# Three shifted sums by accumulating DMA, and three more kv transforms with eight residues

## The chip, the cores and the metric

The kernel runs on one core of a Trainium2 chip. The metric is the device time of one execution in microseconds (us). A core has TensorE (PE: matmuls and transposes, which write to PSUM), VectorE (DVE), ScalarE (ACT) and GpSimd (POOL), each with its own list of instructions, worked off in order, and SyncE (SP), which issues DMAs. DMAs are also issued by ScalarE and GpSimd.

## The reference

A forward pass and all its gradients. `x` is 2048 x 1024, the gated unit has 3584 columns.

```python
k_shift = sum(k_pad[:, t:t + S, :] * shift_k[:, ks - 1 - t] for t in range(4))   # four taps
kv = k_shift * v
y = irfft(rfft(pad(kv)) * rfft(pad(ssm_k))) [:S] + kv * ssm_D                    # long convolution
s = xn * y                                                                       # xn = layernorm(x)
g = silu(((xn @ w_gate) * (xn @ w_up)) @ w_down)
out = x + s * g
# returned: out and the gradients of all nine inputs for a given grad_out
```

What the change touches is the first two lines, the shifted sum `k_shift` and its product with `v`, and the transform of kv.

## The kernel before, in words

The kernel is one long stream for TensorE: layer norm and transposes of x; the gate and up projections in 14 slabs of 256 columns (`gu_unit`, line 655, matmuls at L671); the down projection (L1034); the backward products of the gated unit (L1482, L1499, L1582, L1644). The long convolution runs beside it as a generator, `conv_forward` (line 740), for the forward pass and another for the backward pass. The generator yields after each step, with a weight in us of VectorE's work less most of the TensorE time that the step adds. After each gate-up piece (eight 128x512 matmuls, one PSUM tile `psg`, two buffers) `tick` calls `pump`, which draws steps of the generator until their weights reach the share of a planned total `F_TOTAL` (line 925) that the tick stands for. So the planner's total and the weights set where each step of the convolution stands in the lists of all engines.

The forward convolution works on eight slices `ds` of 128 channels. For each slice there is a *kv* input (16 rows of 128 x 128) and a *filter* input `hx`. Both are transformed by a short transform across residues and matmuls with tables `TF`. A transform consists of two *halves*. A half is a set of matmuls at L234 into two PSUM tiles `psF` (two buffers), which ScalarE copies to a tile `SP` (two buffers, one for each half). VectorE then combines them (`W<-SP` and so on) to the spectrum, `KX` for kv and `HX` for the filter. There are two forms:

- four residues: `fwd4_half`, 16 matmuls of 128x256 a half, ScalarE copies at L256, and on VectorE `fwd4_sums` and `fwd4_outs`, eight operations of 128x1024;
- eight residues: `fwd8_half` (line 287), 8 matmuls of 128x256 a half, ScalarE copies at L295, and on VectorE `fwd8` (line 297), with more sums and four multiply-adds (L283).

`EIGHT` (line 732) lists which transforms take the second form, as pairs of slice and kind (0 is kv, 1 the filter). Slice 0 transforms the filter first, every later slice kv first. A slice then runs so: kv transform, filter transform, turn of the filter spectrum (`turned`), the product of the two spectra (`product`, five steps), the inverse (`inv8` or `inv_dft`), into which the two kv halves of the next slice are laid (`ahead`). The filter halves are laid into the kv transform. The matmuls of the inverse (L455, `psI<-HX,TI`) are laid into the next slice's second transform; those of slice 7 follow the 63rd and the 70th of a counted row of the down projection's matmuls (`late_mm`).

Kv itself is made for two slices at a time by `shift(dp)`, dp from 0 to 3: eight VectorE operations of 128 x 4096 bf16. The sum is in `U[6]`, the product of the moment in `U[7]`, k in `krow`, v in `U[4]`:

```python
tt(acc, k[:, :, 0:8, :], wb(3), MUL)
for j in (2, 1, 0):
    tt(prod, k[:, :, 3 - j:11 - j, :], wb(j), MUL)
    tt(acc, acc, prod, ADD)
tt(kv, acc, v, MUL); st(KSHd[dp], acc)
```

`shift(0)` stands ahead of all slices. `shift(1)`, `shift(2)` and `shift(3)` stand behind the product of slices 1, 3 and 5, and the loads of k and v for them at the start of these slices (`load_kv`, eight DMAs on GpSimd's queue). VectorE's instructions keep the order of the program here (`PIN`). `st` and `cld` issue DMAs from GpSimd, `ld` from SyncE, `sta` from ScalarE. Every VectorE operation by the helper `tt` has line L212, and every store by `st` L66. The other VectorE work of this stage is `hN<-gut`, the product of gate and up, once in four gate-up pieces.

An accumulating DMA is there in one place already: four DMAs of 1 MB at L1550 add A_q to out_0, both in DRAM.

In the backward stage `dw_slab` (line 1495) copies weight gradients to tiles `wb` (three buffers) and stores them.

Of the kernel before, what the change touches and what calls it, by code (L numbers as in the profile page):

```python
# [13 lines left out]
BF16 = mybir.dt.bfloat16  # L14
F32 = mybir.dt.float32
# [4 lines left out]
def build_kernel(  # L20
# [39 lines left out]
    def ld(out, in_):  # L60
        return nc.sync.dma_start(out=out, in_=in_)
# [49 lines left out]
    Hd = dram.tile([NSL, P, 2, NB, P], BF16, name="Hd")  # L111
    HTd = [[dram.tile([4, P, n, 256], BF16, name=f"HTd{i}{j}") for j, n in enumerate((8, 8, 8, 4))] for i in range(2)]
    DGd = dram.tile([NSL, 2, S, SLW], BF16, name="DGd")


    const = ctx.enter_context(tc.tile_pool(name="const", bufs=1))
# [94 lines left out]
    def tt(o, a, b, op):  # L211
        pinned(V.tensor_tensor(o, a, b, op))  # L212
# [439 lines left out]
    chunk = [0]  # L652
    mate = []

    def gu_unit(sl, b0, n, w, tick):

        if n == 4:
            turn_of[0] += 1
            if turn_of[0] % 3 == 0 and sl < NSL - 2:
                gut = U[5][:, 2048:4096].rearrange("p (a i f) -> p a i f", a=2, i=4)  # L660
            else:
                gut = fg.tile([P, 2, 4, SLW], BF16, name="gut")
            hN = fg.tile([P, 2, 4, P], BF16, name="hN", bufs=3)
        else:
            gut = lnp.tile([P, 2, 2, SLW], BF16, name="gut_s", bufs=6)
            hN = lnp.tile([P, 2, 2, P], BF16, name="hN_s", bufs=6)
        for i in range(n):
            q, qi = divmod(b0 + i, 4)
            ps = ps_gu.tile([P, 512], F32, name="psg")
            for dc in range(DC):  # L670
                gu_mm[0] = nc.tensor.matmul(ps[:], XNT[q][:, dc, qi * P:(qi + 1) * P],  # L671
                                            w[:, dc].rearrange("p a f -> p (a f)"), start=(dc == 0), stop=(dc == DC - 1))
            nc.scalar.copy(out=gut[:, :, i], in_=ps[:].rearrange("p (a f) -> p a f", a=2))  # L673
            flush(5)
            if i == 0:
                turn_late()
            hn[0]()
            hn[0] = nop
            tick()
        sta(GUd[sl, b0 // 8][:, :, b0 % 8:b0 % 8 + n], gut[:, :, 0:n])  # L680

        def multiply():
            with tc.issue_after(last.ins) if b0 + n <= 4 and chunk[0] <= 2 else nullcontext():
                by_half = lambda t: t.rearrange("p i (a f) -> p a i f", a=2)
                tt(hN[:, :, 0:n], by_half(gut[:, 0, 0:n]), by_half(gut[:, 1, 0:n]), MUL)
            st(Hd[sl][:, :, b0:b0 + n, :], hN[:, :, 0:n])
            if sl < 2:
                defer(turn)
            else:
                mate.append(hN)  # L690
                if b0 % 8 == 4:
                    defer(turn_pair)
        hn[0] = multiply

        def turn_pair():
            hT = fg.tile([P, 4, 2, 2, P], BF16, name="hT", bufs=1)
            two_, mate[:] = mate[0:2], mate[2:]
            ps = tr_tile()[:].rearrange("p h b x -> p h (b x)").rearrange("p h (b u) -> p h b u", u=64)
            for qq in range(4):
                for a in range(2):  # L700
                    for i in range(2):
                        turn_halves(lambda hh: ps[:, hh, 4 * qq + 2 * a + i], two_[qq // 2][:, a, qq % 2 * 2 + i, :])
            to = HTd[b0 // 8][sl // 4][:, :, 2 * (sl % 4):2 * (sl % 4) + 2, :]
            for g in range(2):
                nc.scalar.copy(out=halves(hT[:, 2 * g:2 * g + 2].rearrange("p q a i s -> p (q a i) s")), in_=ps[:, :, 8 * g:8 * g + 8])
            ht_st[0] = ld(to.rearrange("q f a s -> f q (a s)"), hT[:].rearrange("f q a i s -> f q (a i s)"))

        def store(hT):
            half, rest = divmod(b0, 8)
            q0, i0 = divmod(rest, 2)  # L710
            to = HTd[half][sl // 4][:, :, 2 * (sl % 4):2 * (sl % 4) + 2, :]
            if n == 4:
                ht_st[0] = ld(to[q0:q0 + 2].rearrange("q f a s -> f q (a s)"), hT.rearrange("f q a i s -> f q (a i s)"))
            else:
                ht_st[0] = ld(to[q0, :, :, i0 * P:(i0 + n) * P], hT[:, 0, :, 0:n].rearrange("f a i s -> f a (i s)"))

        def turn():
            hT = fg.tile([P, 4, 2, 2, P], BF16, name="hT", bufs=1)[:, 0:2] if chunk[0] > 5 else lnp.tile([P, 2, 2, 2, P], BF16, name="hT_s", bufs=5)[:]
            ps = tr_tile()[:, 0].rearrange("p (q a i) x -> p q a i x", q=2, a=2)
            for a in range(2):  # L720
# [8 lines left out]
    h_out = []  # L729
    cv_gone = []  # L730
    ht_st = [None]
    EIGHT = ((0, 0), (0, 1), (6, 0), (7, 0), (7, 1))
    INV8 = (2, 4, 5, 6, 7)
    SHIFT_W = 8 * 2.3

# [4 lines left out]
    def conv_forward():  # L740
# [17 lines left out]
        def shift(dp):  # L758
            kv = cx.tile([P, NB, 256], BF16, name="kv")
            S_["kvt", dp] = kv  # L760
            k = S_.pop(("k", dp))
            wb = lambda j: Wbc[:, j:j + 1, dp * 256:(dp + 1) * 256].unsqueeze(1).to_broadcast([P, 2, 8, 256])
            room = cx.tile([P, 16, 256], BF16, name="KX")[:].rearrange("p a x -> p (a x)") if dp == 0 else U[7][:]
            acc, prod, v = [t.rearrange("p (c r d) -> p c r d", c=2, r=8) for t in (U[6][:], room, U[4][:])]
            with tc.issue_after(last.ins):
                tt(acc, k[:, :, 0:8, :], wb(3), MUL)
            yield 2.3
            for j in (2, 1, 0):
                tt(prod, k[:, :, 3 - j:11 - j, :], wb(j), MUL)
                yield 2.3  # L770
                tt(acc, acc, prod, ADD)
                yield 2.3
# [209 lines left out]
    NT = 24 * 8.0 + 33  # L982

    def tick(by=1):
        cnt[0] += by
# [347 lines left out]
    def load_ht(bp):  # L1333
# [2 lines left out]
            last = ld(ht[:, f0:f1], ht_rows(bp, f0, f1))  # L1336
        return (lambda fc: ht[:, fc]), last

    DGU = {}
    wdts = []  # L1340
    wdt_ld = [None]

    def gu_in(k):

        if k < 2 * NSL:
            t = U[(11, 6, 2, 3, 12)[k % 5]][:].rearrange("p (a b f) -> p a b f", b=8, a=2)
            ld(t, GUd[k // 2, k % 2])
            DGU[k] = t

    with tc.issue_after(ht1[1].ins):  # L1350
# [144 lines left out]
    def dw_slab(sl, dgus, others):  # L1495
        for dc in range(DC):
# [15 lines left out]
            next(others, None)  # L1512

    def load_h(sl):
        h = u8(HSL[sl % 3], "p (a b f) -> p a b f", a=2, b=NB)
        ld(h, Hd[sl])
        hs[sl] = h

    for e in later:
        e[0] = -2  # L1520
# [188 lines left out]
    for g in range(1, 4):  # L1709
        for b in (4 * g, 4 * g + 2):  # L1710
            end = b == NB - 2
            pss = [ps_x.tile([P, D], F32, name="psx") for i in range(2)]
            for n in range(12 if end else 14):
# [3 lines left out]
                    DBM[n] = u8((7, 0, 1, 9)[n], a=4)  # L1717
                    ld(DBM[n], DBMd[512 * n:512 * n + 512, :].rearrange("(b u) d -> u b d", u=P))
                if end and n == 4:
                    h = u8(2, "p (a b f) -> p a b f", a=2, b=NB)  # L1720
                    ld(h, Hd[NSL - 1])
                if end and n == 8:
                    ln_loads(NB - 1)
                if g < 3:
# [83 lines left out]
```

## Time and profile before

| | |
|---|---|
| median of 3 runs | 1911.36 us (1911.3 to 1912.02) |
| the profiled execution | 1911.63 us, its span 1909.9 us |
| TensorE matmuls busy | 1899.4 us, 99% of the span |
| VectorE busy | 1549.7 us, 81% |
| forward convolution on VectorE | about 50 to 548 us |
| last gate-up matmul, start of the down projection | 501 us |
| last matmul of the down projection, start of the backward products | 700 us |
| granted clock of TensorE | 1.0 throughout |

The profile shows one execution. Busy time of an engine is the sum of its instructions; a matmul's row shows its whole passage, so eight matmuls that follow each other are better timed from the start of the first to the start of what comes next. The line of 40 digits gives the busy share in slices of 47.7 us. A row such as `U<-k,Wbc 128x4096` names the tile written, the tiles read and the shape; tile numbers are left out. "Idle before" is the time in which the engine stood before an instruction, and the releaser is what it stood for. DMA rows give the time from issue to landing.

### The profile page before, as it was taken

The numbers are of one execution on the slowest core, as the hardware profiler recorded it, in microseconds if no ns is written. First come the engines' busy times: TensorE is split into PE (matmuls) and PEld (weight loads), VectorE is DVE, ScalarE is ACT, GpSimd is POOL, SyncE is SP. The second block draws the span as 40 slices with busy tenths as digits, with TensorE's granted clock in tenths as the row PEclk, the third lists the DMA queues.
The fourth block names the chain that finished last, engine by engine and source line by source line (L and its number), as shares of the span: only waits on it lengthen the run. The fifth ranks groups of instructions, "written<-read, shape, count | busy, mean of one in ns | idle before, by whom it ended". The sixth has DMA issues, their size and how long they took to land.

```text
span 1909.9 us, 28150 instructions
## 1 busy us (share of the span) xinstructions
PE 1899.4 (99%) x11379; PEld 1013.9 (53%) x11379; DVE 1549.7 (81%) x1711; ACT 636.8 (33%) x927; POOL 332.7 (17%) x465
## 2 busy tenths in 40 slices
PE   8999999999999999999999999999999999999999
PEld 5555555545444466666666665664444444444444
DVE  8999999999988556887999999999995305788862
ACT  5765555556333233432222222222222102111121
POOL 5121211201113220001031221211212101111120
PEclk9999999999999999999999999999999999999999
DMA  9777766769769997677897798585887999989852
GB/s 298 269 263 233 251 208 223 252 211 311 241 227 307 316 314 231 209 231 233 264 277 247 231 266 258 184 286 180 230 238 181 219 206 190 194 187 190 194 166 88
DMA packets 425106, 444.34 MB, mean 233 GB/s; under 512 B 268400, under 2 KB 342796, under 8 KB 410512
## 3 DMA queue, kind: packets, MB, share of 16 engines
q1 hardware_dynamic: 367504, 239.03, 45.9%
q0 software_dynamic: 41152, 174.15, 29.0%
q10 hardware_dynamic: 16320, 29.36, 4.1%
q8 instruction: 89, 1.46, 0.3%
q14 instruction: 41, 0.34, 0.1%
HBM read 193.87 MB, written 189.84 MB: 201 GB/s over the span
## 4 chain that ended last, share of the span: by engine, by line
PE 97%; DVE 1%; ACT 1%; DMA 0%; issue 0%; SPq 0%; ACTq 0%
PE psb L1499 20%; PE psx L1644 20%; PE psg L671 19%; PE psb L1482 10%; PE psbm L1034 10%; PE psb L1582 9%; PE psF L234 3%; PE psI L455 1%; PE tr L565 1%; PE psY L1193 1%; PE psY L445 1%; PE psx L1582 1%; DVE bst L578 0%; DMA wslab<-in_B_w_gate_dram 0%; PE tr L788 0%; DVE U L212 0%
## 5 line engine op out<-in xcount | busy, mean ns | idle before, releaser
L671 PE MATMUL psg<-wslab,U 128*128 128x512 bf16 x1792 | 401.8, 379 | 3.5 <-DMA wslab<-in_B_w_gate_dram 2.1
L1499 PE MATMUL psb<-U,U 128*128 128x512 bf16 x1792 | 397.1, 379 | 0.0
L1644 PE MATMUL psx<-U,dgut 128*128 128x512 bf16 x1536 | 332.8, 379 | 0.0
L1644 PEld LDWEIGHTS <-dgut 128*128 128x128 bf16 x1792 | 175.3, 98 | 211.4
L1499 PEld LDWEIGHTS <-U 128*128 128x128 bf16 x1792 | 175.2, 98 | 198.0
L671 PEld LDWEIGHTS <-U 128*128 128x128 bf16 x1792 | 172.6, 98 | 197.2 <-issue 3.6
L1482 PE MATMUL psb<-wdt,U 128*128 128x256 bf16 x1792 | 205.6, 273 | 0.0
L1482 PEld LDWEIGHTS <-U 128*128 128x128 bf16 x1792 | 175.2, 98 | 29.2
L212 DVE TENSOR_TENSOR W<-W 128x1024 f32<-128x1024 f32 (+1 forms) x189 | 186.5, 1003 | 4.1
L1582 PE MATMUL psb<-U,U 128*128 128x512 bf16 x816 | 177.3, 379 | 0.0
L1504 ACT CAST wb<-psb 128x512 bf16<-128x512 f32 x112 | 65.6, 586 | 315.4 <-PE psb L1499 310.5
L1249 DVE SCALAR_TENSOR_TENSOR dkp<-dkT,kT 128x1024 bf16<-128x1024 bf16 (+2 forms) x64 | 78.3, 1223 | 93.1 <-DMA dkT<-DKSHd 91.4
L1034 PE MATMUL psbm<-U,ht 128*128 128x512 bf16 x672 | 146.0, 379 | 0.0
L1582 PEld LDWEIGHTS <-U 128*128 128x128 bf16 x896 | 87.4, 98 | 104.4
L673 ACT CAST gut<-psg 128x512 bf16<-128x512 f32 x156 | 91.5, 589 | 120.2 <-PE psg L671 119.7
L1676 ACT ACTIVATE dx_t<-dxn 128x1024 bf16<-128x1024 f32 x15 | 15.9, 1057 | 324.7 <-DVE dxn L212 324.7
L1034 PEld LDWEIGHTS <-ht 128*128 128x128 bf16 x672 | 65.7, 98 | 78.1
L212 DVE TENSOR_TENSOR U<-U,dht 128x2048 bf16<-128x2048 bf16 x56 | 68.3, 1220 | 46.5 <-ACT dht L1484 46.5
L1484 ACT CAST dht<-psb 128x512 bf16<-128x512 f32 x112 | 65.6, 587 | 116.4 <-PE psb L1482 116.4
L66 POOL DMA_DIRECT2D Hd<-hN x54 | 36.6, 677 | 268.9 <-DVE hN L212 258.9
L1623 ACT CAST wbs<-psb 128x512 bf16<-128x512 f32 x51 | 29.9, 586 | 145.4 <-PE psb L1582 134.3
L212 DVE TENSOR_TENSOR W<-SP 128x1024 f32<-128x1024 f32 x64 | 74.1, 1218 | 1.3 <-ACT SP L295 0.8
(263 smaller groups left out, 2342.9 us busy)
## 6 DMA issues: line engine op xcount, KB each, us to landing
U<-GUd SPq DMA_DIRECT2D x28, 1024.0 KB, 9.3
DGd<-U SPq DMA_DIRECT2D x28, 1024.0 KB, 5.8
GUd<-gut ACTq DMA_DIRECT2D x39, 512.0 KB, 5.2
out_dram<-wb SPq DMA_DIRECT2D x112, 128.0 KB, 4.8
U<-Hd SPq DMA_DIRECT2D x14, 1024.0 KB, 6.6
Hd<-hN POOLq DMA_DIRECT2D x54, 256.0 KB, 4.5
HTd<-hT SPq DMA_DIRECT2D x24, 512.0 KB, 3.7
ht<-HTd SPq DMA_DIRECT2D x18, 512.0 KB, 7.5
```

The source lines that it names most:

```text
L212: pinned(V.tensor_tensor(o, a, b, op))
L234: mm = nc.tensor.matmul(ps[:, k].rearrange("p (c d) -> p c d", c=2), T[:, r, k, :], xr[:, r], start=(n == 0), stop=(n == len(rs) - 1 and ( ...
L671: gu_mm[0] = nc.tensor.matmul(ps[:], XNT[q][:, dc, qi * P:(qi + 1) * P], w[:, dc].rearrange("p a f -> p (a f)"), start=(dc == 0), stop=(dc ...
L673: nc.scalar.copy(out=gut[:, :, i], in_=ps[:].rearrange("p (a f) -> p a f", a=2))
L1034: mm = nc.tensor.matmul(ps[:, dh * 512:(dh + 1) * 512], ht(fc)[:, i * P:(i + 1) * P], WD[fc // 4][:, fc % 4, dh * 512:(dh + 1) * 512], sta ...
L1249: ins = V.scalar_tensor_tensor(prod[:].rearrange("p r d -> p (r d)")[:, lo:H], dkT[:, 0, lo:H], 1.0, kT[:, 0, 13 + m + lo:13 + m + H], op0 ...
L1482: nc.tensor.matmul(ps[:, x * SLW:(x + 1) * SLW], DBMT[2 * hf + g][:, dc, (b % 4) * P:(b % 4 + 1) * P], wdt[:, dc, :], start=(dc == 0), sto ...
L1484: nc.scalar.copy(out=dht[:, 2 * e:2 * e + 2].rearrange("p b f -> p (b f)"), in_=ps[:])
L1499: nc.tensor.matmul(ps[:], XN[b // 4][:, b % 4, dc * P:(dc + 1) * P], dgus[b // 8][:, :, b % 8], start=(b == 0), stop=(b == NB - 1))
L1504: nc.scalar.copy(out=wb[:, dc % 2].rearrange("p a f -> p (a f)"), in_=ps[:])
L1582: nc.tensor.matmul(ps, h[:, f, b, :], DBM[b // 4][:, b % 4, dh * 512:(dh + 1) * 512], start=(b == 0), stop=(b == NB - 1))
L1644: nc.tensor.matmul(ps[:, dh * 512:(dh + 1) * 512], t[n][:, f, i * P:(i + 1) * P], WGU[n][:, f, dh * 512:(dh + 1) * 512], start=(n == 0 and ...
```

## The change

Two things are changed in the forward convolution, and one beside it.

- `EIGHT` gets the kv transforms of slices 2, 3 and 5.
- Shifts 1 to 3 are made by `shift_later`. It has the same four products with the taps and the same last product with v, but the three additions are DMAs issued by GpSimd, from `U[7]` and adding to `U[6]`. Its five steps are spread: in slices 0, 2 and 4 the first two behind the second transform and the third behind the product, and in slices 1, 3 and 5 the fourth behind the first transform and the last (kv, and the store of the sum) behind the second step of the product. K and v are loaded at the start of slices 0, 2 and 4. The planner's total loses the nine additions.
- `wb` has four buffers for three.

The new functions `gut_tile`, `turned_unit` and `h_rows_of` hold a second path for slabs named in `TURNED`, which is empty; for all slabs they do what stood there before.

```diff
-    EIGHT = ((0, 0), (0, 1), (6, 0), (7, 0), (7, 1))
+    EIGHT = ((0, 0), (0, 1), (2, 0), (3, 0), (5, 0), (6, 0), (7, 0), (7, 1))
...
+        def shift_later(dp):
+            kv = cx.tile([P, NB, 256], BF16, name="kv")
+            S_["kvt", dp] = kv
+            k = S_.pop(("k", dp))
+            wb = lambda j: Wbc[:, j:j + 1, dp * 256:(dp + 1) * 256].unsqueeze(1).to_broadcast([P, 2, 8, 256])
+            acc, prod, v = [t.rearrange("p (c r d) -> p c r d", c=2, r=8) for t in (U[6][:], U[7][:], U[4][:])]
+            tt(acc, k[:, :, 0:8, :], wb(3), MUL)
+            yield 2.3
+            for j in (2, 1, 0):
+                tt(prod, k[:, :, 3 - j:11 - j, :], wb(j), MUL)
+                nc.gpsimd.dma_start(out=U[6][:], in_=U[7][:], accum_op=ADD, max_dma_last_dim=4096)
                 yield 2.3
             tt(kv[:].rearrange("p (c r) d -> p c r d", c=2), acc, v, MUL)
             st(KSHd[dp], U[6][:].rearrange("p (b d) -> p b d", b=NB))
...
-            if ds % 2 == 1 and ds < 7:
-                with tc.issue_after(S_["kst"].ins):
+            if ds % 2 == 0 and ds < 6:
+                with tc.issue_after(S_["kst"].ins) if ds else nullcontext():
                     for c in range(2):
                         load_kv(ds // 2 + 1, c)
+                later_kv = shift_later(ds // 2 + 1)
...
+            if ds % 2 == 1 and ds < 7:
+                yield next(later_kv)
             calls = []
...
+            if ds % 2 == 0 and ds < 6:
+                yield next(later_kv)
+                yield next(later_kv)
             if eight:
                 h_rows(ds + 1, 0)
             turned(HX, 1, 0, 1)
...
-            yield from product(KX, HX, KX, cs, False, 0)
+            steps = product(KX, HX, KX, cs, False, 0)
+            yield next(steps)
+            yield next(steps)
             if ds % 2 == 1 and ds < 7:
-                yield from shift(ds // 2 + 1)
+                yield next(later_kv)
+            yield from steps
+            if ds % 2 == 0 and ds < 6:
+                yield next(later_kv)
...
+    F_TOTAL -= 3 * 3 * 2.3
     F_TOTAL += len(EIGHT) * (FWD8_W - 9.6 + 0.95 * 1.75) - 2.0
...
-                wb = bg.tile([P, 2, 2, SLW], BF16, name="wb", bufs=3)
+                wb = bg.tile([P, 2, 2, SLW], BF16, name="wb", bufs=4)
```

More of the change, by code (lines that the diff above doesn't have):

```diff
@@ L113, in build_kernel @@
     DGd = dram.tile([NSL, 2, S, SLW], BF16, name="DGd")
+    TURNED = ()
+    GTd = {sl: dram.tile([2, SLW, S], BF16, name=f"GTd{sl}") for sl in TURNED}
+    HT2d = {sl: dram.tile([SLW, S], BF16, name=f"HT2d{sl}") for sl in TURNED}
     const = ctx.enter_context(tc.tile_pool(name="const", bufs=1))
@@ L653, in build_kernel, with gut_tile, turned_unit, multiply @@
     mate = []
+    def gut_tile(sl):
+        turn_of[0] += 1
+        if turn_of[0] % 3 == 0 and sl >= NSL - 2 and sl in TURNED:
+            return fg.tile([P, 4, 2, 2, P], BF16, name="hT", bufs=1)[:].rearrange("p q a i s -> p (q a i s)").rearrange("p (a i f) -> p a i f", a=2, i=4)
+        if turn_of[0] % 3 == 0 and sl < NSL - 2:
+            return U[5][:, 2048:4096].rearrange("p (a i f) -> p a i f", a=2, i=4)
+        return fg.tile([P, 2, 4, SLW], BF16, name="gut")[:]
+    def turned_unit(sl, b0, w, tick):
+        gut = gut_tile(sl).rearrange("p a i f -> p a (i f)").rearrange("p a (j t) -> p a j t", j=2)
+        hT = fg.tile([P, 2, 4, P], BF16, name="hN", bufs=3)[:].rearrange("p j b s -> p j (b s)")
+        for j in range(2):
+            for a in range(2):
+                ps = ps_gu.tile([P, 512], F32, name="psg")
+                for dc in range(DC):
+                    gu_mm[0] = nc.tensor.matmul(ps[:], w[:, dc, a, j * P:(j + 1) * P], XNT[b0 // 4][:, dc, :],
+                                                start=(dc == 0), stop=(dc == DC - 1))
+                nc.scalar.copy(out=gut[:, a, j], in_=ps[:])
+                flush(5)
+                hn[0]()
+                hn[0] = nop
+                tick(TURNED_TICK)
+        cols = slice(b0 * P, b0 * P + 512)
+        sta(GTd[sl][:, :, cols].rearrange("a (j f) t -> f a j t", f=P), gut)
+        def multiply():
+            flat = lambda t: t.rearrange("p j t -> p (j t)")
+            tt(flat(hT), flat(gut[:, 0]), flat(gut[:, 1]), MUL)
+            st(HT2d[sl][:, cols].rearrange("(j f) t -> f j t", f=P), hT)
+            half, rest = divmod(b0, 8)
+            to = HTd[half][sl // 4][rest // 2:rest // 2 + 2, :, 2 * (sl % 4):2 * (sl % 4) + 2, :]
+            for j in range(2):
+                ht_st[0] = ld(to[:, :, j].rearrange("q f s -> f q s"), hT[:, j].rearrange("p (q s) -> p q s", q=2))
+        hn[0] = multiply
     def gu_unit(sl, b0, n, w, tick):
+        if sl in TURNED:
+            return turned_unit(sl, b0, w, tick)
         if n == 4:
[L658 to L662, printed above, removed]
+            gut = gut_tile(sl)
             hN = fg.tile([P, 2, 4, P], BF16, name="hN", bufs=3)
@@ L771, in shift @@
                 tt(acc, acc, prod, ADD)
+                yield 2.3
+            tt(kv[:].rearrange("p (c r) d -> p c r d", c=2), acc, v, MUL)
+            st(KSHd[dp], U[6][:].rearrange("p (b d) -> p b d", b=NB))
+            yield 2.3
+        def shift_later(dp):
[5 more added lines that the diff above has]
+            tt(acc, k[:, :, 0:8, :], wb(3), MUL)
+            yield 2.3
+            for j in (2, 1, 0):
+                tt(prod, k[:, :, 3 - j:11 - j, :], wb(j), MUL)
+                nc.gpsimd.dma_start(out=U[6][:], in_=U[7][:], accum_op=ADD, max_dma_last_dim=4096)
                 yield 2.3
@@ L981, in build_kernel @@
     cnt = [-5]
-    NT = 24 * 8.0 + 33
+    TURNED_TICK = 1.0
+    NT = 24 * 8.0 + 33 - 16 * len(TURNED) * (1 - TURNED_TICK)
     def tick(by=1):
@@ L1337, in load_ht, with h_rows_of @@
         return (lambda fc: ht[:, fc]), last
+    def h_rows_of(sl, t):
+        if sl in TURNED:
+            h = t[:].rearrange("p (b f) -> p b f", b=NB)
+            for half in range(2):
+                nc.sync.dma_start_transpose(out=h[:, 8 * half:8 * half + 8], in_=HT2d[sl][:, 1024 * half:1024 * half + 1024])
+            return h.rearrange("p b (a f) -> p a b f", a=2)
+        h = t[:].rearrange("p (a b f) -> p a b f", a=2, b=NB)
+        ld(h, Hd[sl])
+        return h
     DGU = {}
@@ L1346, in gu_in @@
             t = U[(11, 6, 2, 3, 12)[k % 5]][:].rearrange("p (a b f) -> p a b f", b=8, a=2)
-            ld(t, GUd[k // 2, k % 2])
+            sl, hf = divmod(k, 2)
+            if sl in TURNED:
+                for a in range(2):
+                    nc.sync.dma_start_transpose(out=t[:, a], in_=GTd[sl][a][:, 1024 * hf:1024 * hf + 1024])
+            else:
+                ld(t, GUd[sl, hf])
             DGU[k] = t
@@ L1514, in load_h @@
     def load_h(sl):
-        h = u8(HSL[sl % 3], "p (a b f) -> p a b f", a=2, b=NB)
-        ld(h, Hd[sl])
-        hs[sl] = h
+        hs[sl] = h_rows_of(sl, U[HSL[sl % 3]])
     for e in later:
@@ L1719, in build_kernel @@
                 if end and n == 4:
-                    h = u8(2, "p (a b f) -> p a b f", a=2, b=NB)
-                    ld(h, Hd[NSL - 1])
+                    h = h_rows_of(NSL - 1, U[2])
                 if end and n == 8:
```

## The prediction

> **What bounds the kernel now.** I read the page first (busy time, slices, chain), then the windows of the forward stage, then who waited there, then the two engines' timelines, and last the rows of DMAs that resemble the new ones. All times are us from the start of the span.
>
> ```profile
> PE 1899.4 (99%) x11379; PEld 1013.9 (53%) x11379; DVE 1549.7 (81%) x1711; ACT 636.8 (33%) x927; POOL 332.7 (17%) x465
> PE   8999999999999999999999999999999999999999
> DVE  8999999999988556887999999999995305788862
> PE 97%; DVE 1%; ACT 1%; DMA 0%; issue 0%; SPq 0%; ACTq 0%
> ```
>
> TensorE is busy for 1899.4 of 1909.9 us and makes up 97% of the chain that ended last: a matmul less is time less, as long as nothing makes TensorE wait in its place. But VectorE is full in slices 2 to 11 too, just where this change lies. The windows show how full (columns: PE, PEld, DVE, ACT, POOL busy, then clock, DMA share, GB/s):
>
> ```profile
> 290.00:320.00 30.00, 29.41 (x213) 17.64 (x211) 29.79 (x23) 18.78 (x25) 4.12 (x6) 1.00 0.57 196
> 410.00:440.00 30.00, 30.00 (x223) 16.20 (x222) 29.69 (x34) 18.86 (x26) 2.01 (x3) 1.00 0.59 204
> 530.00:560.00 30.00, 30.00 (x149) 14.35 (x148) 21.89 (x26) 8.38 (x10) 0.00 (x0) 1.00 0.59 209
> ```
>
> Until the forward convolution ends near 548 both engines run at 99 to 100%; behind it VectorE has holes. So a matmul saved here counts only if VectorE gets no more work. From 200 to 700 TensorE waited once:
>
> ```profile
> PE psF L234 <- DVE kv L212: 0.6, 1, 0.6
> ```
>
> That is the half transform of slice 4, at 297.47, standing ready until the shift's last product (kv) was written. The two engines are timed against each other to within a microsecond there. The other end of the stage has room (first a line of VectorE's timeline, then two of TensorE's):
>
> ```profile
> 546.06 2.50 DVE L283 SCALAR_TENSOR_TENSOR HX<-W 128x512 bf16<-128x512 f32 x4
> ```
>
> ```profile
> 492.69 1.04 PE L234 MATMUL psF<-hx,TF 128*128 128x256 bf16 x8
> 493.57 3.62 PE L671 MATMUL psg<-wslab,U 128*128 128x512 bf16 x16
> ...
> 554.95 1.04 PE L455 MATMUL psI<-HX,TI 128*128 128x256 bf16 x8
> ```
>
> VectorE's last write of the inverse input (HX) ends at 548.5; TensorE reads it at 554.95, a place fixed behind a counted number of the down projection's matmuls. That is 6.4 us of **margin**.
>
> **Part 1: eight residues for kv of slices 2, 3 and 5.** A half transform issues 16 matmuls with four residues and 8 with eight; a transform has two halves. The pair of lines above prices eight at 493.57 - 492.69 = 0.88 us a half. Four:
>
> ```profile
> 339.75 1.91 PE L234 MATMUL psF<-kv,TF 128*128 128x256 bf16 x16
> 341.50 5.34 PE L671 MATMUL psg<-wslab,U 128*128 128x512 bf16 x24
> ```
>
> 341.50 - 339.75 = 1.75 us. Saved on TensorE: 3 x 2 x (1.75 - 0.88) = **5.2 us**, all on the path. ScalarE copies the same two tiles per half either way, so it is unchanged. VectorE pays:
>
> ```profile
> 358.03 4.63 DVE L212 TENSOR_TENSOR W<-SP 128x1024 f32<-128x1024 f32 x4
> 362.57 4.62 DVE L212 TENSOR_TENSOR KX<-W 128x1024 bf16<-128x1024 f32 x4
> 367.12 0.68 DVE L212 TENSOR_TENSOR hN<-gut 128x1024 bf16<-128x1024 bf16 x1
> ...
> 427.93 4.63 DVE L212 TENSOR_TENSOR W<-SP 128x1024 f32<-128x1024 f32 x4
> ...
> 444.99 4.63 DVE L212 TENSOR_TENSOR W<-SP 128x1024 f32<-128x1024 f32 x4
> ```
>
> Four residues (slice 5): 367.12 - 358.03 = 9.1 us. Eight (slice 6): 444.99 - 427.93 = 17.06, less two hN products of 0.6 each that lie in it = 15.9 us. Three times the difference of 6.8 is +20.3 us of VectorE.
>
> **Part 2: the additions of shifts 1, 2 and 3 go to DMAs.** Nine 128x4096 additions leave VectorE. The whole of shift 3, eight such operations, runs from 390.99 to 410.90, which is 19.9, less three hN of 0.6 = 18.1, so 2.26 each; nine are **-20.4 us**. VectorE's balance is -0.1 us: nothing. Its forward work still ends near 548.5, while TensorE comes to the inverse 5.2 us earlier. Of the margin of 6.4 about 1.2 us are left, and that is what is late next.
>
> **Part 3: the new waits.** Each accumulating DMA reads the product (U7) and rewrites the sum (U6). The next product may not be written until the DMA before it has landed, and the last product (kv) not before the third. VectorE runs in program order, so whatever stands behind the product waits as well: the rest of the slice, then ScalarE's copies of SP, then TensorE. What lies between:
>
> - first to second DMA: the turn of the filter spectrum and the whole product. In the same place of slice 4 that runs from 326.81 to 341.00: 14.2 us, hN included.
> - second to third: an inverse and a transform; in slices 0 and 1 from 119.43 to 138.99: 19.6, and more where an eight-residue transform or inverse stands.
> - third to kv: a filter transform, the turn and two steps of the product; in slice 1 from 139.59 to 155.19: 15.6.
>
> The nearest row is the four DMAs that add A_q to out_0, of the same size and also accumulating, but between DRAM tensors:
>
> ```profile
> L1550 POOL DMA_DIRECT2D out_dram<-in_A_q_dram x4: 966/986/1022, 796.2 to 933.1; - x4
> DMA to landing us min/median/max: 11.9/13.7/14.9
> ```
>
> They met DMA shares near 1.0; the forward windows show 0.57 to 1.00. The lower bound is the plain 1 MB store KFd<-KX, 5.2 us at the median. I take 11 to 14, near the accumulating row: it fits into 14.2. At the row's 14.9 each of three first gaps is 0.7 short, 2.1 us together, of which 1.2 are covered. The issue itself costs POOL 9 x 1.0 us of an engine 17% busy.
>
> The Trainium skill ("DMA: Bandwidth & Descriptors", section "Anatomy of one DMA — SWDGE (gpsimd) path") fits a DMA issued there as 2.0 us plus its bytes over 436 GB/s, an estimate of 4.4 us for 1 MB. By it the gaps are never short, the 1.0 us below falls away and rival 2 has no chance. The rows here, 11.9 to 14.9, disagree with it under load and with accumulation, so I keep them.
>
> **Part 4: order.** kv is now written before the last three steps of the product, not after the shift. That is 7 us earlier against TensorE's half, so the 0.6 us wait should go: -0.6. The loads of k and v are issued at the start of slices 0, 2 and 4: eight DMAs per slice, landing in 9 to 12 us (rows k 10.9 and 8.8, U<-in_A_v 10.3). They are wanted two transforms later, 18.9 us (192.88 to 211.77 in slice 2); that is their cover. Without it VectorE would wait the difference. On POOL's queue they stand ahead of the h stores, which nobody on the path waits for. The planner's total rises from 431.5 to 439.2 (three times 9.46 less 20.7) over the same ticks, so the steps of the convolution come 1.8% denser to the gate-up pieces; TensorE's list changes by position, not by count.
>
> **At nothing.** A fourth wb buffer: ScalarE waited 2.9 us for out_dram<-wb, hidden behind four psb banks (psb L1499 waited 0.0); without that cover it would be a gain of at most 2.9. gut_tile, h_rows_of and the turned paths: TURNED is empty, so the same instructions are issued.
>
> **The sum** on the profiled run (1911.63, of which 1909.9 span): -5.2 - 0.6, and +1.0 for new waits, taken between 0 (gaps long enough) and 1.5 (14.9 landings plus what is left of the margin once the 0.6 is gone too). That is -4.8, 1906.8. The median of the runs lies 0.3 below the profiled run, so **1906.6**.
>
> **Rivals.**
>
> 1. *TensorE runs into VectorE in the middle* (1909.7). TensorE gains 5.2 us by slice 5, VectorE nothing, so TensorE's lead grows. A filter half is issued while VectorE still reads the SP buffers of the kv half before it: in slice 4 VectorE's second W<-SP pair ends at 312.27 and ScalarE's copy into that buffer starts at 313.25, in slice 5 at 362.57 and 363.69. The lead may grow by 1.0 and 1.1 us there; what goes beyond makes ScalarE wait, and through psF and psg (two buffers each) TensorE. If the list stays as it is, the gain is capped at that 1.1 and the 0.6 of kv: 1911.36 - 1.7 = 1909.7. For it: ScalarE already waited four times, 3.0 us, for W<-SP. Against it: TensorE's list breaks gate-up groups around halves (six matmuls, a half, ten matmuls at 361 to 365), so there is other work to put in front. At its worst, with the waits of part 3 on top, nothing is gained and 1 us is lost.
> 2. *The accumulating DMA is late* (about 1924, slower). Price: three first gaps and three last ones. With a landing of L the excess is 3(L - 14.2) + 3(L - 15.6), less about 1 of margin; at L = 16 it equals the gain, from 16.6 on the kernel is over 0.2% slower, at 18 it loses 17.6 and gains 5.2: 1923.8. For it: the filter store of 1 MB is issued right behind the first DMA, and POOL can stand 4.2 us at an h load that waits for TensorE's transposes ahead of it. Against it: 14.9 was the longest of the row, at fuller DMA engines.
> 3. *No new wait at all* (1905.6). The DMA lands as fast as the plain store, 5.2, and the rest of the sum stands. For it: the SBUF to SBUF path is not in the rows; against it: the accumulating row.
>
> **Chances.** Forecast with rival 3's fast form 0.58; rival 1 0.25; rival 2 0.12; anything else 0.05, half of it slower. A measurement of this kernel can tell about 0.2%, 3.8 us, from no change: below 1907.5 is faster, above 1915.2 slower. Faster 0.60, same 0.26, slower 0.14. The range takes the forecast and rival 1: from 1904.0 (no new wait, 1905.6, less 0.7 by which the runs differ and 0.9, a third of what the wb buffer could give) to 1912.4 (rival 1 at its worst).
>
> **What would show it.** Part 1: psF<-kv falls from 208 to 160 matmuls, busy PE by 5 us. Part 2: U<-U,U (nine of 128x4096) is gone from VectorE, and its last HX write stays within a microsecond of 548. Part 3: an idle VectorE ahead of U<-k or kv with the DMA U<-U as the releaser is rival 2; its landing below 14 is my case. Part 4: no wait of psF for kv. Rival 1 would be waits of psF or psg on ScalarE between 300 and 500. I am wrong most simply if VectorE's products slow down while those DMAs run, for which no row here has a case. The Trainium skill ("SBUF — State Buffer", section "Who interferes with whom") holds that a DMA has ports of its own and never contends with a compute engine; by it that cannot happen, and no run so far shows it.

## The result and the profile after

The changed kernel took 1915.88 us (median of 12 runs, 1913.96 to 1921.62), the kernel before 1911.45 (12 runs, 1911.30 to 1912.26): a ratio of 1.0026, 95% interval 1.0018 to 1.0033. It is slower by about 0.26%, where 1906.6 was forecast; 1915.88 lies above the range's upper end of 1912.4. Two single executions far off all others, one of experiment 6 (2197.69 us, at a granted clock of 0.851) and one of experiment 9 (7143.48 us), are left out of the medians below.

The profiled execution of the changed kernel took 1914.6, its span 1912.8, so 2.9 more than the span before (1909.9). First the lines of its page that answer to those of before: busy time, slices, chain.

```profile
PE 1895.4 (99%) x11331; PEld 1008.9 (53%) x11331; DVE 1548.6 (81%) x1738; ACT 637.2 (33%) x927; POOL 346.1 (18%) x474
PE   8999999999999999999999999999999999999999
DVE  8999999999988556887999999999995205788862
PE 95%; DMA 3%; ACT 1%; DVE 1%; SPq 0%; issue 0%; ACTq 0%
```

TensorE issues 48 matmuls fewer and is busy 4.0 us less; VectorE's total is the same within 1.1. VectorE is as forecast; of TensorE's 5.2 us, 1.2 are missing. What is new is in the last line: DMA now makes up 3% of the chain that ended last, where it had 0%.

The window of 290 to 320 us (PE, PEld, DVE, ACT, POOL busy, clock, DMA share, GB/s) shows it too; before it is in the prediction:

```profile
290.00:320.00 30.00, 29.20 (x227) 16.56 (x226) 26.46 (x23) 17.25 (x24) 6.23 (x8) 1.00 0.91 302
```

At 290 to 320 the DMA engines went from 0.57 to 0.91 of their time, VectorE, full before, has 3.5 us of holes, and TensorE 0.8. TensorE's waits (us in total, times, longest) give the price:

```profile
PE psg L708 <- ACT U L710: 5.2, 2, 4.7
...
PE psF L237 <- ACT SP L259: 0.8, 1, 0.8
```

Neither line was there before, and the wait for kv (0.6) is gone. Line 708 is the gate-up matmul (671 before), 710 ScalarE's copy of its result. The chain of work around the longest of them (start, us, what):

```profile
169.77 18.11 DMA HTd<-hT
...
187.96 1.93 ACT hT L742 x2
189.88 1.83 ACT SP L298 x2
191.72 0.50 ACT U L710
...
192.26 3.51 PE psg L708 x8
```

Read it from the top. SP's store of the turned h, HTd<-hT (512 KB), takes 18.1 us to land; its median was 3.7 before and is 4.7 now. The tile hT has one buffer, so ScalarE's next copy into it waits, 4.8 us here. The row of ScalarE's waits (us in total, times, longest), which before did not have:

```profile
ACT hT L742 <- DMA HTd<-hT: 8.5, 4, 4.8
```

ScalarE works in order: the copies of SP and of the gate-up result stand behind it. psg has two buffers, both full, and TensorE stops for 4.7 us. At 296 to 315 the same happens on a smaller scale: an HTd store that takes 15.7, ScalarE 1.4 late, VectorE 3.3, TensorE 0.8.

Why was the store late? GpSimd's timeline (start, us, instruction, and in brackets the idle time before it and its releaser):

```profile
158.66 0.58 POOL L66 DMA_DIRECT2D KSHd<-U  x1 [6.99 <-DMA U<-U]
...
162.48 0.90 POOL L66 DMA_DIRECT2D k<-in_A_k_dram  x1
167.60 0.71 POOL L66 DMA_DIRECT2D Hd<-hN  x1 [4.21 <-DVE hN L215]
168.19 0.65 POOL L66 DMA_DIRECT2D k<-in_A_k_dram  x1
168.72 1.66 POOL L66 DMA_DIRECT2D U<-in_A_v_dram  x2
```

The store of the shifted kv (KSHd) has to wait for the third accumulating DMA, and holds GpSimd for 7.0 us. Behind it come the loads and stores of the slice and seven of the eight loads of k and v for the next shift, all between 158 and 178; most of the loads stand behind a second wait too, 4.2 us for hN. The loads come here as soon as their tiles are free (the first at 150.06, ahead of KSHd), not at their place in slice 2. What that does to the queues is in the DMA view of 165 to 180 (queue: packets, MB, share of the 16 engines); q0 is GpSimd's, q1 is SP's. Before:

```profile
q0 software_dynamic: 205, 0.64, 12.3%
q1 hardware_dynamic: 545, 0.53, 10.7%
```

After:

```profile
q0 software_dynamic: 1028, 4.30, 75.3%
q1 hardware_dynamic: 1004, 0.51, 12.3%
```

The two queues got about equal numbers of packets, 1028 and 1004; but a packet of GpSimd's has 4.2 KB here and one of SP's 0.5 KB. The Trainium skill ("DMA: Bandwidth & Descriptors", section "Queues, rings and completion order") says that each DMA engine takes the queues in turn, a packet each; if its packets are those that the profile counts, the equal counts agree. Turns are not all of it: from 296 to 300, SP's queue holds the HTd store issued at 295.88, and the DMA view shows no packet of that queue beside 147 of GpSimd's. What holds it there is not shown.

The 1004 packets are not the store's own, however. SP's queue also carries the loads of the weight slab (wslab). Two of them were issued at 154.64 and 155.06, ahead of the store of 169.77, and landed late (the DMA view of 150 to 190; the last figure is us to landing):

```profile
wslab<-in_B_w_up_dram SPq DMA_DIRECT2D x1, 512.0 KB, 20.7
wslab<-in_B_w_gate_dram SPq DMA_DIRECT2D x1, 512.0 KB, 31.5
```

The second landed at 186.6 and the store at 187.9, right behind it. The sizes of the packets say the same. From 155 to 160, when the HTd store issued at 150.80 is first in SP's queue, they have 1 KB (242 packets, 0.25 MB); from 165 to 180 they have 0.5 KB, so they are the slab's. The store's own packets ran from 180 on. Until then it stood in its own queue, behind loads that GpSimd's traffic had slowed down. Before the change the slab loads of this place took 7.2 and 9.7 us, and the store 3.6.

The sum of the 2.9 us of span: -5.2 (matmuls) and -0.6 (kv wait), +5.2 and +0.8 (the two waits), +1.2 (5.2 less the 4.0 by which busy TensorE fell; matmuls slowed behind the long wait, below), and a remainder of +1.5. About 1.1 of it is lost in the first 100 us, where TensorE is busy 91.97 instead of 93.61 and 0.5 of the difference is the shorter psg wait. Some 0.5 is lost by 40 us already, before the forward convolution begins.

### The profile page after: what moved, and what is told of

It is laid out like the page before. It is cut to its first block, busy times and chain, and to the rows that moved or that the text cites. A ratio compares the mean times of both kernels' runs of the same rounds, so it can differ in the third digit from the quotient of the medians.

```text
span 1912.8 us, 28081 instructions
## 1 busy us (share of the span) xinstructions
PE 1895.4 (99%) x11331; PEld 1008.9 (53%) x11331; DVE 1548.6 (81%) x1738; ACT 637.2 (33%) x927; POOL 346.1 (18%) x474
## 4 chain that ended last, share of the span: by engine, by line
PE 95%; DMA 3%; ACT 1%; DVE 1%; SPq 0%; issue 0%; ACTq 0%
PE psx L1723 20%; PE psb L1580 20%; PE psg L708 17%; PE psb L1563 10%; PE psbm L1100 10%; PE psb L1661 9%; PE psF L237 2%; DMA HTd<-hT 2%; PE psI L458 1%; PE psY L1259 1%; PE tr L568 1%; PE psY L448 1%; PE psx L1661 1%; DMA wslab<-in_B_w_gate_dram 1%; DVE bst L581 0%; PE tr L841 0%
## 5 line engine op out<-in xcount | busy, mean ns | idle before, releaser
L215 DVE TENSOR_TENSOR W<-W 128x1024 f32<-128x1024 f32 (+1 forms) x198 | 194.4, 997 | 4.3
```

## Experiments

Three theories went in. **B**: the loads of k and v in one bunch hold up SP's store. **C**: the accumulating DMAs' own traffic does. **L**: TensorE, 5.2 us lighter, merely runs into the others. Line numbers are those of the changed kernel unless a kernel shifts them by two.

**1. The DMAs and the order without part 1** (e1_only_acc).

```
-    EIGHT = ((0, 0), (0, 1), (2, 0), (3, 0), (5, 0), (6, 0), (7, 0), (7, 1))
+    EIGHT = ((0, 0), (0, 1), (6, 0), (7, 0), (7, 1))
```

> The accumulating shifts as in the changed kernel, but the five eight-residue transforms of before. TensorE has its 5.2 us back and VectorE 20 us less. Theory B (bunched loads: the loads of k and v, now issued as soon as krow and v are free, meet the stores of the slice, slow the stores of hT and with them ScalarE and TensorE): the same bunch, so the wait of ScalarE for HTd<-hT stays and the time is that of the changed kernel plus 5.2, 1919 to 1921. Theory C (the accumulating DMAs' own traffic): the same, 1919 to 1921. Theory L (TensorE's lead of 5.2 us over VectorE is what makes it wait): no lead, no wait, 1910 to 1912.

Measured: 1920.68 (5 runs, 1917.27 to 1923.02), ratio 1.0045 [1.0033, 1.0058]. TensorE does not run ahead here, and still waits (from 60 us on):

```profile
PE psg L708 <- ACT U L710: 6.3, 4, 2.8
PE psg L708 <- ACT gut L710: 2.0, 2, 1.8
```

L is refuted as the cause of the waits.

**2. Without the accumulating DMAs** (e3_no_acc): line 824 removed; the sums of shifts 1 to 3 lack three of their four terms.

```
-                nc.gpsimd.dma_start(out=U[6][:], in_=U[7][:], accum_op=ADD, max_dma_last_dim=4096)
```

> The changed kernel without its nine accumulating DMAs: the three later shifted sums lack three of their four terms. Nothing else differs, and VectorE has the same work. Theory C: the waits for HTd<-hT go, 1905 to 1907. Theory B: the loads still meet the stores, with less backlog before them, so part of the wait stays, 1908 to 1914. Theory L: nothing changes, 1915.

Measured: 1907.89 (1907.05 to 1910.18), ratio 0.998 [0.9971, 0.9989]; from 60 us on TensorE waits 0.7 us for ScalarE, at most 0.5 at a time, and between 100 and 200 us the DMA share is 0.71 instead of 0.86.

**3. Without the loads** (e5_no_loads): k and v are not loaded again for shifts 1 to 3, which work on those of shift 0.

```
             S_["k", dp] = krow
+            if dp > 0:
+                return
```

> The changed kernel without the loads of k and v for shifts 1 to 3 (they use those of shift 0, so these slices' results are not the reference's). Theory B: the waits go, 1905 to 1907. Theory C: 1912 to 1915, since the accumulating DMAs are all there. Theory L: 1914 to 1916.

Measured: 1907.97 (1907.18 to 1909.85), ratio 0.998 [0.9971, 0.9989]. Taking away either one gives the same time. The long wait of TensorE is gone in both traces (at most 0.5 and 0.4 us are left from 60 us on). So neither B nor C alone is the cause: the wait needs both.

**4. The same loads, later** (e4_late_loads): those of shifts 2 and 3 are held in GpSimd's queue until the newest h store has been issued.

```
-                with tc.issue_after(S_["kst"].ins) if ds else nullcontext():
+                with tc.issue_after(hd_st[0].ins) if ds else nullcontext():
```

> The changed kernel with the loads of k and v for shifts 2 and 3 held back behind the newest store of hN, some 20 us later, when the stores of the slice have landed; all work is there. Theory B: no wait for HTd<-hT near 190 and 310, 1905.5 to 1908.5. Theory C: no difference beyond 1 or 2 us, 1914 to 1916. Theory L: 1914 to 1916. If the loads now come too late VectorE waits for k.

Measured: 1908.57 (1906.96 to 1909.67), ratio 0.9982 [0.9973, 0.999]. The loads of shift 2 are now issued at 186 to 192, and the chain from 165 to 215 holds nothing but TensorE; two pieces of it:

```profile
168.90 8.74 PE psg L710 x40
...
185.25 5.25 PE psg L710 x24
```

Not one byte was taken away. From 165 to 180 GpSimd's queue moves 3.47 MB instead of 4.30. The slab loads ahead of the store landed within 20.9 us instead of 31.5, and no HTd store between 160 and 200 took longer than 8.9 us. VectorE does not wait for k behind 100 us: the last of it landed at 201.5, the first product of shift 2 starts at 211.9. This kernel does all the work and is faster than the changed kernel and the one before. The longest wait of TensorE that is left behind 50 us is one of 1.8 us at 85 us, in slice 0.

**5. The first shift's loads late too** (e6_all_late).

```
-                with tc.issue_after(hd_st[0].ins) if ds else nullcontext():
+                with tc.issue_after(hd_st[0].ins) if hd_st[0] else nullcontext():
```

> The late loads again, with the loads of the first later shift (slice 0) also held until the newest h store has been issued; all work is there. Theory B (the loads of k and v, issued in one bunch, starve the HTd store beside the other traffic): the one wait of TensorE for ScalarE that is left with late loads, 1.84 us at 85, stands behind slice 0's loads, so it goes, and the time falls by 1 to 2 us to 1906.6-1907.6. Theory C (the accumulating DMAs' own traffic): no such DMA has been issued before 110 us, so it is not their doing either way and nothing is said of 85 us; 1908.6. A loss would mean that the loads now come late for the shift: VectorE idle ahead of the first product with the load of k as the releaser, up to 10 us, 1912-1918.

Measured: 1908.97 (1907.87 to 1913.63), ratio 0.999 [0.9981, 0.9999]. The edit moved the first of these loads from 65.9 to 72.3 only, so it says little of B: the HTd store issued at 74 still took 6.9. TensorE's waits for ScalarE behind 50 us fell from 2.5 us to 1.6 all the same, and the time did not fall.

**6. The first shift's loads between slice 0's two transforms** (e9_between), beside late loads in slices 2 and 4:

```
             if ds % 2 == 1 and ds < 7:
                 yield next(later_kv)
+            if ds == 0:
+                with tc.issue_after(hd_st[0].ins):
+                    for c in range(2):
+                        load_kv(1, c)
+                later_kv = shift_later(1)
```

> The late loads, with the loads of the first later shift moved between the two transforms of slice 0 (holding them at the slice's start until the newest h store moved them by 6 us only, and 1908.97 against 1908.57 said nothing of theory B); all work is there. Theory B (loads in one bunch starve the HTd store, ScalarE stands at hT, TensorE behind it): the store issued at 74 us then runs beside no load, the 1.84 us wait of TensorE at 85 us goes, and the time is 1906.5-1907.5. It may turn up 15 us later, behind the next HTd store, if the bunch only moves: then 1908.5 as before. If VectorE has to wait for k (shift's first product at 106), 1910 or more.

Measured: 1908.55 (1907.54 to 1909.59), ratio 0.998 [0.9971, 0.9989]. The mechanism answered as B says: with the loads at 89.8 to 96.3 the HTd store of 74.7 landed in 2.8 us instead of 9.2, and TensorE's waits for ScalarE fell from 2.5 us to 1.0 behind 50 us. The time did not: in the profiled run a lead of 1.6 us over the late loads at 116 is 0.7 at 502, and the medians are equal. That last wait is worth less than the runs differ.

**7. Late loads, without part 1** (e7_late_five): the EIGHT of before, as in experiment 1.

> The late loads with the EIGHT of before (five transforms with eight residues instead of eight): the additions by DMA and the new order alone, without the bunch. If the 5.2 us of part 1 are all on the path, this is 5.2 slower than the late loads' 1908.6: 1913.8, no better than before. By rival 1 of the prediction (TensorE runs into VectorE, the gain is capped near 1.7) it is only 1 to 2 us slower: 1909.6-1910.3. VectorE has 20 us less work here, so it should have holes of that size between 200 and 548.

Measured: 1921.67 (5 runs, 1920.10 to 1923.27), ratio 1.0054 [1.004, 1.0068]. Against experiment 4 that is 13.1 slower, not 5.2 and not 1 to 2. In the profiled runs 11.2 us of span lie between them: busy TensorE is 1900.7 against 1894.6, so 6.1 are matmuls (the granted clock is 1.0 in both), and TensorE's waits for ScalarE behind 50 us are 7.2 against 2.5. One of these is new and not near any accumulating DMA (the last was issued at 379):

```profile
PE psg L710 <- ACT gut L712: 3.0, 1, 3.0
```

It stands at 466, behind a gut store that took 12.7 us beside the stores HFd and YFd and the loads of w_down. So part 1 is worth its matmuls and more here; why the order with five falls on a bad moment at 466 is not settled. Nor do the late loads gain anything with five such transforms: 1921.67 here, 1920.68 in experiment 1. That holding the loads back helps is shown for the changed kernel only.

**8. Plain copies in place of the accumulating ones** (e8_plain_copy): same tiles, same 4 KB packets; the additions of shifts 1 to 3 are left out.

```
-                nc.gpsimd.dma_start(out=U[6][:], in_=U[7][:], accum_op=ADD, max_dma_last_dim=4096)
+                nc.gpsimd.dma_start(out=U[6][:], in_=U[7][:], max_dma_last_dim=4096)
```

> The changed kernel, whose nine accumulating DMAs are plain copies U7 to U6 of the same tiles in the same packets: the sums of shifts 1 to 3 leave the additions out. It tells what the adding costs on the DMA engines. If it is the adding (a read of the target beside the write), the 1 MB copies take about half of the accumulating DMAs' engine time, landing 5 to 8 us, the wait of TensorE for ScalarE at 190 shrinks from 4.7 to under 2 us, and the time falls to 1909-1911. If it is 1 MB more of any kind in the bunch, landings and waits stay as they are: 1913-1916.

Measured: 1909.73 (1907.64 to 1913.22), ratio 0.9988 [0.9979, 0.9997]. The copies landed faster than the additions (8.4/9.7/12.7 in the changed kernel):

```profile
DMA to landing us min/median/max: 4.9/6.1/8.4
```

The KSHd store then held GpSimd for at most 5.2 us instead of 7.1, and the 4.7 us wait of TensorE is gone. So 6.2 us (1915.88 - 1909.73) of the 8.0 that the DMAs cost in all (1915.88 - 1907.89) are the adding itself, not 1 MB more (6.6 of 8.4 when each is set against the kernel before of its own series). KSHd's wait at 155 is 3.3 us here, and seven of the eight loads still go out between 163 and 175; but the slab loads landed within 22.2 us instead of 31.5, and the HTd store behind them took 13.0 instead of 18.1.

**9. The additions in 1 KB packets** (e13_small_acc): `max_dma_last_dim=1024` in line 824.

> The changed kernel, its nine accumulating DMAs cut into packets of 1 KB instead of 4 KB; the same bytes, all work is there. It asks by what the HTd store loses beside the software queue. If queues are served a packet each in turn, shorter packets beside it give SP's 0.5 KB packets a larger share while an accumulating DMA runs: HTd's store issued at 170 us lands in under 14 us instead of 18, TensorE's wait at 190 is under 2 us, and the time is 1910-1913, although the accumulating DMAs themselves land later, 12 to 16 us. If only the engine time that the DMAs take counts, 1024 packets with their own cost each take longer than 256, all of it gets worse: landings of 15 us or more, VectorE waiting for U<-U, 1918-1926.

Measured: 1917.32 (11 runs, 1909.55 to 1921.54), ratio 1.0022 [1.001, 1.0034]. Landings went from 9.7 to 11.6 (15.8 at the longest), the HTd store of 170 to 19.7, TensorE's longest wait from 4.7 to 6.2. The time lies between the two forecasts, and its interval overlaps that of the changed kernel (1.0018 to 1.0033). Smaller packets did not help, but the test was weaker than meant: no accumulating DMA is under way between 160 and 190, where the store stood, only what had been held up behind one.

**10. Part 1 alone** (e2_only_eight): the kernel before with eight residues for slices 2, 3 and 5, additions on VectorE.

```
-    EIGHT = ((0, 0), (0, 1), (6, 0), (7, 0), (7, 1))
+    EIGHT = ((0, 0), (0, 1), (2, 0), (3, 0), (5, 0), (6, 0), (7, 0), (7, 1))
...
-    NT = 24 * 8.0 + 33
+    NT = 24 * 8.0 + 28
```

> The kernel before with the EIGHT of the changed one alone (kv of slices 2, 3 and 5 with eight residues, additions on VectorE, loads where they were); the planner's number of ticks is 28 over 24 x 8 instead of 33, so that the convolution's forward part is out in time. TensorE saves 5.2 us, VectorE gets 20.3 us more. By the prediction's balance (both engines full from 100 to 548, a margin of 6.4 us at the inverse of slice 7) TensorE must wait for what exceeds the margin: 20.3 + 5.2 - 6.4 = 19.1, less the 5.2, so 13.9 slower: 1920-1926. If VectorE is not that tight, the gain stands alone: 1906-1908.

Measured: 1937.14 (4 runs, 1936.60 to 1937.91), ratio 1.0133 [1.0118, 1.0147]. VectorE's busy time is 20.4 higher, as priced. TensorE waits mostly where the prediction looked for it:

```profile
PE psF L234 <- DVE kv L212: 9.9, 3, 5.2
PE psF L234 <- ACT SP L295: 4.8, 1, 4.8
```

It loses 11 us more than the upper end of what was expected: behind such waits the clock fell (0.97 to 0.98 in four of the 100 us windows), so that TensorE is busy 1902.7 us with the same 11331 matmuls for which the late loads needed 1894.6. Without the additions gone from VectorE, part 1 is a loss (with this number of ticks; no other was run).

**11. Three wb buffers** (e10_late_wb3): the late loads with `bufs=3` for wb.

> The late loads with three wb buffers, as before the change, instead of four. The prediction priced the fourth buffer at nothing, at most 2.9 us where the four psb banks do not cover ScalarE's wait for out_dram<-wb. Nothing: 1907.5-1909.5 with ScalarE waiting some 3 us for out_dram<-wb and TensorE not at all. If the buffer is worth something: 1910-1911.5, with TensorE waiting for psb.

Measured: 1908.43 (1907.44 to 1912.99), ratio 0.9986 [0.9977, 0.9995]. The fourth buffer is worth nothing: ScalarE waits 2.9 us for out_dram<-wb, TensorE never for psb.

Nearly all of the difference is there at the end of the gate-up projections. The last gate-up store of all stands at 501.97 in the kernel before; against that, and against its span:

| kernel | last gate-up store | span |
|---|---|---|
| changed | +2.6 | +2.9 |
| 1 without part 1 | +11.2 | +11.3 |
| 2 no accumulating DMAs | -5.4 | -4.6 |
| 3 no loads | -4.9 | -4.5 |
| 4 late loads | -3.0 | -2.8 |
| 8 plain copies | -1.1 | -1.1 |
| 10 part 1 alone | +24.7 | +25.5 |

## Why the prediction was wrong

**Part 1** was right: 48 matmuls gone (psF<-kv from 208 to 160), 5.9 us less busy TensorE in experiment 2 (1893.5 against 1899.4) where 5.2 was said, and +20.4 of VectorE in experiment 10 where +20.3 was said.

**Part 2** was right in the balance (VectorE 1549.7 to 1548.6). The end of its forward work came later than 548.5 in the changed kernel, since VectorE itself had waited for SP (8.4 us in all, 0.8 before). VectorE's last write of HX and TensorE's first read:

```profile
550.92 2.50 DVE L286 SCALAR_TENSOR_TENSOR HX<-W 128x512 bf16<-128x512 f32 x4
```

```profile
557.54 1.04 PE L458 MATMUL psI<-HX,TI 128*128 128x256 bf16 x8
```

The margin is 557.54 - 553.42 = 4.1, not 1.2, because TensorE was late as well; with late loads it is 5.3 (546.7 to 552.0). It decided nothing.

**Part 3** was right on what it asked. The accumulating DMA's landing:

```profile
L824 POOL DMA_DIRECT2D U<-U x9: 1192/1211/1229, 110.5 to 389.9; - x9
...
DMA to landing us min/median/max: 8.4/9.7/12.7
```

It stayed below 14, mostly under the 11 to 14 that was taken, and VectorE never waited for one; the +1.0 was not needed. The fear that VectorE's products slow down beside such DMAs was empty: U<-k,Wbc took 2288 ns on average against 2285. The rule of the Trainium skill ("SBUF — State Buffer", section "Who interferes with whom") held here. The other rule of the Trainium skill in this part ("DMA: Bandwidth & Descriptors", section "Anatomy of one DMA — SWDGE (gpsimd) path", 4.4 us estimated) is too low for additions: 9.7, against 6.1 for a plain copy in the same place. What part 3 left out was the engine that issues them. It priced GpSimd at 9 x 1.0 us of issue and not at the wait of KSHd for the third landing, 19.5 us over three shifts, with the slice's stores and the next loads queued behind it. That wait by itself does no harm, though: it is 21.5 us with late loads and 23.4 without the loads, and both kernels are faster than the one before. How much of the bunch it makes is not shown.

**Part 4** is the step that failed. It said of the loads of k and v: "On POOL's queue they stand ahead of the h stores, which nobody on the path waits for." It looked for harm on their own queue and for cover against their own user, VectorE. The harm was on another queue: from 165 to 180 GpSimd's long packets take 75% of the DMA engines and SP's queue 12%. The slab loads in SP's queue land late, the HTd store behind them later still, and on that store hang hT's one buffer, ScalarE, psg and TensorE. The prediction put this at nothing; it cost 4.7 us of waiting at 188 and the slowed matmuls behind it. It also took the loads to be issued at their place in the slice, where they went out as soon as their tiles were free, next to the stores that KSHd had held up. Its -0.6 for kv was right. No run gave hT a second buffer or moved the slab loads, so whether breaking the chain there would do as well is open.

**The sum** without this step nearly holds: -4.8 was forecast, and experiments 2 and 3, from which one half of the traffic is missing, are at -4.0 (1907.89 and 1907.97 against 1911.9), the late loads at -3.3. The changed kernel is at +4.4. So the missing term is about 8 us, in the profiled run 5.2 + 0.8 of waits and 1.2 of clock. The late loads' span stays 3.0 us behind -5.8, and 2.5 of it are waits of TensorE for ScalarE, most of it at 85 us; but with those down to 1.0 (experiment 6) 2.7 were still missing, so this remainder is not settled.

**Rivals.** Rival 1 did not happen: ScalarE's waits for W<-SP (3.0 us before) are gone, and experiment 7 is 13.1 behind experiment 4 where it allowed 1 to 2. Rival 2 had the right cause, a late landing, and the wrong victim: not VectorE through U7, but TensorE through GpSimd's and SP's queues. Rival 3 (1905.6) had no new wait, with a landing of 5.2 us: the additions landed in 9.7, but no operation of VectorE waited for them. Once the bunch is taken apart the time is 1907.9 to 1908.6, above it and above the forecast.

## What to carry to other kernels

When a change adds or moves DMAs, ask which transfers on other queues are under way in the same microseconds, and which of them fill or free a tile with a single buffer. Their median landing is no price there: one store went from 3.6 to 18.1 us, because the loads ahead of it in its own queue had been slowed down too. Hold back what is not urgent. Here the loads of two shifts needed only another place in the queue, and a loss of 0.26% became a gain of 0.18%; with five transforms (experiment 7) the same move gained nothing.

## What the runs showed of the hardware

A short stop of TensorE can cost more than its length. The matmuls behind the 4.7 us wait, and the window that holds them (the clock is the third figure from the end):

```profile
192.26 3.51 PE L708 MATMUL psg<-wslab,U 128*128 128x512 bf16 x8 [4.68 <-ACT U L710]
```

```profile
192.20:195.60 3.40, 3.34 (x8) 1.13 (x8) 3.37 (x4) 0.50 (x2) 0.00 (x0) 0.50 1.07 276
```

Eight of these take 1.89 us elsewhere in this timeline; here the granted clock is 0.50 for 3.4 us. In experiment 1 a wait of 2.81 was followed by 16 matmuls in 5.30 us; in experiment 4, after 1.84, they took 3.61. The Trainium skill ("TensorE: Matmul & The Clock Gate", Part 1) ties the clock to how busy TensorE has lately been, which agrees. The length of a stop alone does not decide: in experiment 7 waits of 3.20 and 3.04 us were not followed by slower matmuls (16 in 3.61, 24 in 5.34, granted clock 1.0). In the traces of experiments 1, 9 and 10 too, the slow stretches last 3.4 us or twice that. One reading that fits: the clock is set by how much of a fixed stretch of 3.4 us was idle. Counted back from the slow stretch, the wait of 2.81 leaves 2.3 us of one such stretch empty; counted on from the trace's first clock record, those of 3.20 and 3.04 are each split over two, with at most 2.0 empty in one. No run tested it, and idle time is not all of it: in experiment 10 a stretch with 1.7 us empty was followed by a slow one.

A 1 MB addition within SBUF by DMA landed in 9.7 us at the median where a plain copy took 6.1; its 4 KB packets took about 0.38 us each instead of about 0.2 (first DMA of each, at 110).

The runs of the changed kernel spread over more (1914.0 to 1921.6) than those of the kernel before in the same series (1911.3 to 1912.3) and those with late loads (1907.0 to 1909.7). That waiting for DMAs makes the spread is not shown: the late loads with three wb buffers range from 1907.4 to 1913.0.
